# Retention and a low-rank mixer on one core: the low-rank expansion in four row tiles, later scores in batch 2, a later load of U

## The chip, the cores and the metric

The kernel runs on one core of one Trainium2 chip. The time is the device time of one execution in microseconds. The kernel before takes 241.34 us, the median of three runs (241.11 to 241.67).

## The reference, cut to what matters

There are 4 batches, 8 heads, 768 tokens and a head dimension of 64, so a token has 512 values. First comes a retention: each head has a state that decays by a factor of its own at each token, takes in the outer product of k and v, and is read with q. The heads side by side are x. Then a low-rank mixer works across tokens (U is 768 x 32, V is 32 x 768), and a feed-forward works on each token:

```python
state = gamma * state + einsum('bhd,bhe->bhde', k[:, :, t], v[:, :, t])
y[:, :, t] = scale * einsum('bhd,bhde->bhe', q[:, :, t], state)
# x: y with the heads side by side, (4, 768, 512)
h = x.transpose(0, 2, 1) @ U @ V
u = x + h.transpose(0, 2, 1)
out = u + np.maximum(u @ w_ch1, 0.0) @ w_ch2      # 512 -> 2048 -> 512
```

Inputs and output are float32.

## The kernel before, in words

**Retention.** The kernel takes the tokens in chunks of 128. GpSimd scales q and k of a chunk by powers of the decay and casts to bf16 (prep_chunk, L240 to L253). The chunk is turned so that the head dimension lies on partitions: for batch 1 by TensorE and a copy by ScalarE (turn_pe, L376), for batches 2 and 3 by one DMA transpose through the crossbar, issued from ScalarE's queue (turn_dma, L387 to L392; tile qkT). Then state (L394) updates the running state, score (L413) makes the products of q and k in two PSUM banks with the tag s, VectorE multiplies them with the causal mask (L422), and mix (L425) sums them with v and with the state into bank o, which ScalarE copies out as x. Score needs the turned chunk, mix needs both masked tiles. Batch 0 has a version of its own, before everything else.

**The low-rank part.** lr_proj (L450) multiplies x with U, giving for each of four column blocks c of 128 values a product of 32 x 128. The four lie on partitions 32c to 32c+31 of one tile, pc, which VectorE copies out of bank o. lr_expand (L460 to L470) multiplies it with V, block by block: for a token block j and a column block c it is one matmul with 32 rows of contraction (L464), and its row tile in the array is c. Before the change, a call does two column blocks, into two banks with the tag s, and then VectorE adds x to each bank (L468), giving u. A second call does the other two column blocks; it takes the same two banks, so it waits until VectorE has read them. u is turned for the feed-forward into uT, for batches 0 and 1 by TensorE (lr_turn_pe, L472, two token blocks at a time through bank qk, copied by ScalarE), except that blocks 0 to 3 of batch 0 are made directly at L632; for batches 2 and 3 by the crossbar (lr_turn, L481 to L484). Names in the trace: u_752, u_1515, u_2183 and u_2810 are batches 0 to 3.

**Feed-forward, and the order.** The feed-forward of a batch is a list of 56 pieces of four matmuls each (mlp_pieces, L496): 16 up pieces for tokens 0 to 511 (L507, priced 0.864), 16 up pieces for tokens 512 to 767 (priced 0.432), and 24 down pieces, four to each token block (L530, 0.864). The prices sum to 41.47. Up pieces end in a relu, the third of every three on VectorE, the others on ScalarE. While the feed-forward of batch b-1 is written out, the retention and the low-rank part of batch b are put between its pieces by weave (L551): each step has a mark, a share of the 41.47, and goes ahead of the first piece that begins at or after it. The marks are in L653 to L680: chunk i has a mark at[i], and turn, state, score and mix come at[i], at[i] + lag[0], + lag[1] and + lag[2]. After the last mix come projection, the expansion of token blocks 0 to 3, and their turns; blocks 4 and 5 follow at the start of the next batch (first, L638 and L650). Each engine runs its instructions in the order of this program.

**PSUM.** There are eight banks (L63): one each for the tags qk, o and st, two for s, three for the feed-forward.

**Loads.** All loads go through the sync queue in the order of the list feed (L138 to L155), 16 ahead of their use. U is needed twice, in a pair-wise order of tokens for batch 0 and in natural order for the others; the second (key u2) is loaded after the up weights, and prep_u2 (L263) has GpSimd cast U and copy V for it, ahead of batch 1's first chunk.

Of the kernel before, what the change touches and what calls it, by code (L numbers as in the profile page):

```python
# [17 lines left out]
def kernel(  # L18
# [11 lines left out]
    nc = tc.nc  # L30
    P = 128
# [6 lines left out]
    NCB = DM // P  # L38
# [26 lines left out]
    def bank(tag, dtype=fp32):  # L65
        n_bank[0] += 1
        return psum.tile([P, 2048 // (4 if dtype == fp32 else 2)], dtype,
                         tag=tag, name=f"{tag}_{n_bank[0]}", bufs=BANKS[tag])

    def four(t):  # L70
        return t.rearrange("p (n m) -> p n m", n=4)
# [21 lines left out]
    feed = []  # L93
# [3 lines left out]
    def feed_chunk(b, ci):  # L97
        for nm, src in (("q", q), ("k", k), ("v", v)):
            feed.append(((nm, b, ci),
                         src[b, :, ts(ci, P), :].rearrange("h p d -> p h d")))  # L100
# [8 lines left out]
    def feed_one():  # L109
        if n_fed[0] == len(feed):  # L110
            return
        key, src = feed[n_fed[0]]
        n_fed[0] += 1
        if key[0] == "uv":
            for i in range(2):
                nc.sync.dma_start(
                    out=Uf[0][ds(HP * i, HP)],
                    in_=moe_U.rearrange("(j p two) r -> two p j r", p=HP,
                                        two=2)[i])
            for c in range(NCB):  # L120
                nc.sync.dma_start(out=Vf[ds(RK * c, RK)], in_=moe_V)
            return
        if key[0] == "u2":
            nc.sync.dma_start(out=Uf[1],
                              in_=moe_U.rearrange("(j p) r -> p j r", p=P))
            return
        t = rin.tile([P, 512], fp32, tag="in", name=f"in_{n_fed[0]}")
        ready[key] = t
        if key[0] in "qkv":
            t = t.rearrange("p (h d) -> p h d", h=H if len(key) == 3 else 4)  # L130
        nc.sync.dma_start(out=t, in_=src)  # L131

    def take(*key):
        assert feed[n_used[0]][0] == key, (feed[n_used[0]][0], key)
        n_used[0] += 1
        return ready.pop(key, None)
# [4 lines left out]
    for mb in range(4):  # L141
        for c in range(NCB):
            feed.append((("w1", mb, c), moe_w_ch1[ts(c, P), ts(mb, 512)]))
    feed.append((("u2",), None))
    for ci in range(AHEAD):
        feed_chunk(1, ci)
    for m in range(NM):
# [1 line left out]
    for b in range(1, B):  # L149
        for ci in range(NCK):  # L150
            if b > 1 or ci >= AHEAD:
                feed_chunk(b, ci)
    for _ in range(RING):
        feed_one()

# [6 lines left out]
    def keep_busy(n, fresh=False):  # L162
        if fresh:
            idle_bank[0] = bank("mlp")
        for _ in range(n):
            nc.tensor.matmul(idle_bank[0], ones[:, :P], ones, start=True,  # L166
                             stop=True, skip_group_check=True)
# [43 lines left out]
    for i in range(NST):  # L211
        t = consts.tile([P, 4, P], bf16, name=f"state{i}")
# [27 lines left out]
    def prep_chunk(b, ci):  # L240
        qkd = rpre.tile([P, 2, H, D], bf16, tag="qkd", name=f"qkd_{b}_{ci}")
        vd = rpre.tile([P, H, D], bf16, tag="vd", name=f"vd_{b}_{ci}")
        pre[b, ci] = qkd, vd
        for t, nm, g in ((qkd[:, 0], "q", gq), (qkd[:, 1], "k", gk),
                         (vd, "v", None)):
            src = take(nm, b, ci).rearrange("p (h d) -> p h d", h=H)
            if g is None:
                nc.gpsimd.tensor_copy(out=t, in_=src)
            else:
                nc.gpsimd.tensor_tensor(  # L250
                    t, src, g[:, ci, :, None].to_broadcast([P, H, D]),
                    op=ALU.mult)
            feed_one()  # L253
# [9 lines left out]
    def prep_u2():  # L263
        take("u2")
        nc.gpsimd.tensor_copy(out=Ub[1], in_=Uf[1])
        nc.gpsimd.tensor_copy(out=V4[1], in_=Vf)
        feed_one()

    def prep_w1(mb):
        for c in range(NCB):  # L270
            nc.gpsimd.tensor_copy(out=w1b[:, c, ts(mb, 512)],
                                  in_=take("w1", mb, c))
            feed_one()
# [170 lines left out]
    us, uTs, pcs = {}, {}, {}  # L444
# [12 lines left out]
        pcs[b] = rmid.tile([P, P], bf16, tag="pc", name=f"pc_{b}")  # L457
        evac("D", pcs[b], p_p[:, :P])

    def lr_expand(b, c0, j0, nj):  # L460
        banks = [bank("s") for _ in range(2)]
        for j in range(j0, j0 + nj):
            for c in (c0, c0 + 1):
                nc.tensor.matmul(banks[c - c0][:, ts(j - j0, P)],  # L464
                                 V4[b > 0][ds(RK * c, RK), ts(j, P)],
                                 pcs[b][ds(RK * c, RK)], start=True, stop=True)
        for c in (c0, c0 + 1):
            nc.vector.tensor_tensor(  # L468
                us[b][:, ds(j0, nj), ts(c, P)], four(banks[c - c0])[:, :nj],
                xs[b][:, ds(j0, nj), ts(c, P)], op=ALU.add)  # L470

    def lr_turn_pe(b, j0):  # L472
# [78 lines left out]
    def weave(pieces, *tracks):  # L551
        total = sum(c for c, _ in pieces)
        marks = []
        for steps, start, end in tracks:
            for i, f in enumerate(steps):
                marks.append((total * (start + (end - start) * i / len(steps)),
                              f))
        marks.sort(key=lambda m: m[0])
        at = 0.0
        for cost, f in pieces:  # L560
            while marks and marks[0][0] <= at:
                marks.pop(0)[1]()
            late = len(stores)
            f()
            for _ in range(late):
                store()
            at += cost
        for _, f in marks:
            f()
        while stores:  # L570
            store()

    def part(f, *args):
        return lambda: f(*args)
# [4 lines left out]
    def x_turn(c):  # L579
        xT[c] = bank("mlp" if c < 3 else "s")  # L580
        for j in range(NLO):
            nc.tensor.matmul(xT[c][:, ts(j, P)], xs[0][:, j, ts(c, P)], ident,
                             start=(j == 0), stop=False, skip_group_check=True)
# [34 lines left out]
    mix_block(NSC - 1, "AD")  # L618
    for mb in range(4):
        prep_w1(mb)  # L620
    prep_u2()
    x_turn(3)
    idle_bank[0] = bank("s")
    keep_busy(2)
# [10 lines left out]
    for c in range(NCB):  # L635
        evac("AD"[c % 2], uTs[0][:, :NLO, c], four(xT[c]))
    keep_busy(3)
    first = [part(lr_expand, 0, 0, 4, 2), part(lr_expand, 0, 2, 4, 2),  # L638
             part(lr_turn_pe, 0, 4),
             part(lr_expand, 0, 0, 0, 4),  # L640
             part(lr_expand, 0, 2, 0, 4)]

    for ci in range(AHEAD):
        prep_chunk(1, ci)
# [2 lines left out]
    for b in range(1, B + 1):  # L647
        tracks = []
        if b > 1:
            first = [part(lr_expand, b - 1, 0, 4, 2),  # L650
                     part(lr_expand, b - 1, 2, 4, 2),
                     part(lr_turn_pe if b == 2 else lr_turn, b - 1, 4)]
        tracks.append((first, 0.02, 0.2))  # L653
        if b < B:
            if b == 1:
                at = [0.5, 0.6, 0.655, 0.715, 0.77, 0.825]
                lag = [0.01, 0.035, 0.065]
                turn = turn_pe
                for i in range(AHEAD, NCK):
                    tracks.append(([part(prep_chunk, b, i)], at[i] - 0.1, 1))  # L660
            else:
                for i in range(NCK):
                    prep_chunk(b, i)
                at = [0.06 + 0.11 * i for i in range(NCK)]
                lag = [0.1, 0.12, 0.2]
                turn = turn_dma
            for i in range(NCK):
                for f, d in ((turn, 0), (state, lag[0]), (score, lag[1]),
                             (mix, lag[2])):
                    tracks.append(([part(f, b, i)], at[i] + d, at[i] + d))  # L670
            t = at[-1] + lag[2]
            tracks += [([part(lr_open, b), part(lr_proj, b)], t + 0.02, t + 0.02),
                       ([part(lr_expand, b, 0, 0, 4),
                         part(lr_expand, b, 2, 0, 4)], t + 0.035, t + 0.055)]
            if b == 1:
                tracks.append(([part(lr_turn_pe, b, 0), part(lr_turn_pe, b, 2)],
                               t + 0.07, t + 0.09))
            else:
                tracks.append(([part(lr_turn, b, 0), part(lr_turn, b, 2)],
                               t + 0.075, t + 0.076))  # L680
        weave(mlp_pieces(b - 1), *tracks)
# [29 lines left out]
```

## Time and profile before

| what | value |
|---|---|
| time, median of three runs | 241.34 us |
| span of the profiled execution | 240.2 us |
| TensorE matmul busy | 224.9 us, 94% |
| TensorE weight loads, beside matmuls | 123.3 us, 51% |
| VectorE busy | 96.5 us, 40% |
| ScalarE busy | 86.7 us, 36% |
| GpSimd busy | 81.2 us, 34% |
| moved by DMA | 39.18 MB, mean 163 GB/s |

Busy shares are means over stages with different limits. TensorE is the engine that is nearly always busy, so its gaps and what ends them are to be looked for; a gap on another engine costs nothing unless TensorE waits for it. In the lines of the profile, a time in brackets is the engine's idle time ahead of an instruction, with what ended it. Batch 0's retention takes the first 28 us, its feed-forward up to about 87, that of batch 1 up to about 142, of batch 2 to about 194, and of batch 3 to the end.

### The profile page before, as it was taken

Reading aid. Unit: us, or ns where it says so; the run is one execution under the profiler, and the core shown is the slowest. Engines: PE = TensorE matmul, PEld = TensorE weight load, DVE = VectorE, ACT = ScalarE, POOL = GpSimd, SP = SyncE. Lnnn points to the kernel's source line nnn. Section 1 sums busy time; section 2 is a strip of 40 time slices with the busy share of each in tenths; the row PEclk is TensorE's granted clock in tenths of the full one; section 3 lists DMA queues with packets and bytes.
Section 4 is the critical chain, followed back from the end, with each engine's and each line's share of the span. In section 5 each row is a group of like instructions: output and inputs, shape, how many; then the busy total and the mean of one; then the engine's idle time right before and its main releaser. Section 6 shows DMA issues by size and latency. Waiting matters only on the chain.

```text
span 240.2 us, 4801 instructions
## 1 busy us (share of the span) xinstructions
PE 224.9 (94%) x1936; PEld 123.3 (51%) x1936; DVE 96.5 (40%) x179; ACT 86.7 (36%) x175; POOL 81.2 (34%) x121
## 2 busy tenths in 40 slices
PE   7898999999999779997989999999999999999993
PEld 3466544685565334465544434568444434584441
DVE  5577445323435523443333524444334533321221
ACT  3266453455463045554320004566210024460000
POOL 5542879688676664264644100000000000000000
PEclk9999999999999999999999999999999999999999
DMA  6997999999999999999999163422331342001112
GB/s 181 295 293 187 277 343 257 364 315 227 216 221 213 235 216 258 212 163 227 170 262 196 46 147 71 90 44 49 84 91 46 87 132 46 0 0 46 72 59 87
DMA packets 94630, 39.18 MB, mean 163 GB/s; under 512 B 78096, under 2 KB 87312, under 8 KB 94608
## 3 DMA queue, kind: packets, MB, share of 16 engines
q1 hardware_dynamic: 73008, 29.43, 54.1%
q10 hardware_dynamic: 21600, 9.44, 16.9%
q8 instruction: 15, 0.25, 0.4%
q14 instruction: 7, 0.06, 0.1%
HBM read 27.85 MB, written 6.29 MB: 142 GB/s over the span
## 4 chain that ended last, share of the span: by engine, by line
PE 74%; DMA 14%; DVE 3%; ACT 2%; SPq 2%; issue 2%; POOL 1%; ACTq 0%; DVEq 0%; POOLq 0%
DMA qkT_2_1830<-qkd_2_1633 3%; DMA in_186<-in_v_dram 3%; DMA qkT_4_2015<-qkd_4_1655 3%; DMA in_106<-in_q_dram 2%; SPq L131 2%; PE mlp_1375 L530 2%; PE mlp_2776 L530 1%; PE mlp_2149 L530 1%; PE mlp_2672 L530 1%; PE mlp_1273 L530 1%; PE mlp_1179 L530 1%; PE mlp_2637 L530 1%; PE mlp_1095 L530 1%; PE mlp_3215 L530 1%; PE mlp_3155 L530 1%
## 5 line engine op out<-in xcount | busy, mean ns | idle before, releaser
L507 PEld LDWEIGHTS <-w1b 128*128 128x128 bf16 x512 | 48.0, 98 | 33.4 <-issue 1.4
L530 PEld LDWEIGHTS <-gT_2906 128*128 128x128 bf16 x96 | 9.4, 98 | 11.1
L530 PEld LDWEIGHTS <-gT_1677 128*128 128x128 bf16 x96 | 8.7, 98 | 9.6
L530 PEld LDWEIGHTS <-gT_2313 128*128 128x128 bf16 x96 | 8.7, 98 | 9.6
L530 PEld LDWEIGHTS <-gT_852 128*128 128x128 bf16 x96 | 8.2, 98 | 7.2
L166 PE MATMUL mlp_199<-ones 128*128 128x512 bf16 x24 | 8.0, 478 | 1.4 <-DVE ones L159 1.4
L166 PEld LDWEIGHTS <-ones 128*128 128x128 bf16 x40 | 3.8, 110 | 5.7 <-issue 2.3
L464 PEld LDWEIGHTS <-V_84 32*128 32x128 bf16 x72 | 2.2, 92 | 7.1 <-issue 7.1
L514 ACT ACTIVATE gT_2906<-mlp_2907 128x512 bf16<-128x512 f32 x1 | 0.6, 597 | 10.8 <-PE mlp_2907 L507 10.8
L514 ACT ACTIVATE gT_2313<-mlp_2314 128x512 bf16<-128x512 f32 x1 | 0.6, 597 | 10.7 <-PE mlp_2314 L507 10.7
L530 PE MATMUL mlp_1375<-w2b,gT_852 128*128 128x512 bf16 x16 | 4.1, 380 | 0.0
L530 PE MATMUL mlp_1179<-w2b,gT_852 128*128 128x512 bf16 x16 | 4.1, 380 | 0.0
L530 PE MATMUL mlp_1452<-w2b,gT_852 128*128 128x512 bf16 x16 | 4.1, 380 | 0.0
L530 PE MATMUL mlp_2212<-w2b,gT_1677 128*128 128x512 bf16 x16 | 4.0, 381 | 0.0
L530 PE MATMUL mlp_2839<-w2b,gT_2313 128*128 128x512 bf16 x16 | 4.0, 381 | 0.0
L530 PE MATMUL mlp_1544<-w2b,gT_852 128*128 128x512 bf16 x16 | 4.0, 380 | 0.0
L530 PE MATMUL mlp_2045<-w2b,gT_1677 128*128 128x512 bf16 x16 | 4.0, 380 | 0.0
L530 PE MATMUL mlp_2672<-w2b,gT_2313 128*128 128x512 bf16 x16 | 4.0, 380 | 0.0
L530 PE MATMUL mlp_1273<-w2b,gT_852 128*128 128x512 bf16 x16 | 4.0, 380 | 0.0
L530 PE MATMUL mlp_1095<-w2b,gT_852 128*128 128x512 bf16 x16 | 4.0, 380 | 0.0
L530 PE MATMUL mlp_2149<-w2b,gT_1677 128*128 128x512 bf16 x16 | 3.8, 380 | 0.0
L530 PE MATMUL mlp_2776<-w2b,gT_2313 128*128 128x512 bf16 x16 | 3.8, 380 | 0.0
(906 smaller groups left out, 549.4 us busy)
## 6 DMA issues: line engine op xcount, KB each, us to landing
Vf<-in_moe_V_dram SPq DMA_DIRECT2D x4, 96.0 KB, 4.1
in_90<-in_k_dram SPq DMA_DIRECT2D x1, 256.0 KB, 3.0
in_92<-in_k_dram SPq DMA_DIRECT2D x1, 256.0 KB, 3.4
in_94<-in_q_dram SPq DMA_DIRECT2D x1, 256.0 KB, 4.4
in_96<-in_q_dram SPq DMA_DIRECT2D x1, 256.0 KB, 4.7
in_98<-in_v_dram SPq DMA_DIRECT2D x1, 256.0 KB, 5.1
in_100<-in_v_dram SPq DMA_DIRECT2D x1, 256.0 KB, 5.4
in_102<-in_k_dram SPq DMA_DIRECT2D x1, 256.0 KB, 5.7
```

Of the source, the lines that this page charges most:

```text
L131: nc.sync.dma_start(out=t, in_=src)
L166: nc.tensor.matmul(idle_bank[0], ones[:, :P], ones, start=True, stop=True, skip_group_check=True)
L464: nc.tensor.matmul(banks[c - c0][:, ts(j - j0, P)], V4[b > 0][ds(RK * c, RK), ts(j, P)], pcs[b][ds(RK * c, RK)], start=True, stop=True)
L507: nc.tensor.matmul(g_p[:, :sz], w1b[:, c, ts(m, P)], uTs[b][:, ds(j, nj), c], start=(c == 0), stop=(c == NCB - 1))
L514: nc.scalar.activation(gT[:, m, ds(lo, sz)], g_p[:, :sz], AF.Relu)
L530: nc.tensor.matmul(ch, gT[:, m, ts(j, P)], w2b[:, m], start=(m == 0), stop=(m == NM - 1))
```

## The change

There are three edits, and the number of instructions of each kind stays the same.

The low-rank expansion does all four column blocks in one call. Its matmuls go to four row tiles of the array in turn and write four banks: the two of tag s, and those of o and qk. The purpose is that four row tiles can work side by side and that no call has to wait for the banks of the one before it. The VectorE adds follow one another.

For batch 2 the lags are larger: state at 0.12, score at 0.17 and mix at 0.21 behind the turn, in place of 0.10, 0.12 and 0.20. The purpose is to have the scores of batch 2 come later behind the crossbar transposes that they read. Everything behind the last mix of this batch has its mark 0.01 later.

The natural-order U is loaded behind the chunks of batch 1, and its casts on GpSimd stand behind the last chunk of batch 1 instead of ahead of the first.

```diff
-    feed.append((("u2",), None))
     for ci in range(AHEAD):
         feed_chunk(1, ci)
...
             if b > 1 or ci >= AHEAD:
                 feed_chunk(b, ci)
+        if b == 1:
+            feed.append((("u2",), None))
...
-    def lr_expand(b, c0, j0, nj):
-        banks = [bank("s") for _ in range(2)]
+    def lr_expand(b, j0, nj):
+        banks = [bank(t) for t in ("s", "s", "o", "qk")]
         for j in range(j0, j0 + nj):
-            for c in (c0, c0 + 1):
-                nc.tensor.matmul(banks[c - c0][:, ts(j - j0, P)],
+            for c in range(NCB):
+                nc.tensor.matmul(banks[c][:, ts(j - j0, P)],
                                  V4[b > 0][ds(RK * c, RK), ts(j, P)],
                                  pcs[b][ds(RK * c, RK)], start=True, stop=True)
-        for c in (c0, c0 + 1):
+        for c in range(NCB):
             nc.vector.tensor_tensor(
...
-    prep_u2()
...
-    first = [part(lr_expand, 0, 0, 4, 2), part(lr_expand, 0, 2, 4, 2),
-             part(lr_turn_pe, 0, 4),
-             part(lr_expand, 0, 0, 0, 4),
-             part(lr_expand, 0, 2, 0, 4)]
+    first = [part(lr_expand, 0, 4, 2), part(lr_turn_pe, 0, 4),
+             part(lr_expand, 0, 0, 4)]
...
+                tracks.append(([prep_u2], at[-1] - 0.05, 1))
...
-                lag = [0.1, 0.12, 0.2]
+                lag = [0.12, 0.17, 0.21] if b == 2 else [0.1, 0.12, 0.2]
...
-                       ([part(lr_expand, b, 0, 0, 4),
-                         part(lr_expand, b, 2, 0, 4)], t + 0.035, t + 0.055)]
+                       ([part(lr_expand, b, 0, 4)], t + 0.035, t + 0.035)]
```

More of the change, by code (lines that the diff above doesn't have):

```diff
@@ L458, in lr_proj @@
         evac("D", pcs[b], p_p[:, :P])
-    def lr_expand(b, c0, j0, nj):
-        banks = [bank("s") for _ in range(2)]
+    def lr_expand(b, j0, nj):
+        banks = [bank(t) for t in ("s", "s", "o", "qk")]
         for j in range(j0, j0 + nj):
-            for c in (c0, c0 + 1):
-                nc.tensor.matmul(banks[c - c0][:, ts(j - j0, P)],
+            for c in range(NCB):
+                nc.tensor.matmul(banks[c][:, ts(j - j0, P)],
                                  V4[b > 0][ds(RK * c, RK), ts(j, P)],
                                  pcs[b][ds(RK * c, RK)], start=True, stop=True)
-        for c in (c0, c0 + 1):
+        for c in range(NCB):
             nc.vector.tensor_tensor(
-                us[b][:, ds(j0, nj), ts(c, P)], four(banks[c - c0])[:, :nj],
+                us[b][:, ds(j0, nj), ts(c, P)], four(banks[c])[:, :nj],
                 xs[b][:, ds(j0, nj), ts(c, P)], op=ALU.add)
@@ L649 @@
         if b > 1:
-            first = [part(lr_expand, b - 1, 0, 4, 2),
-                     part(lr_expand, b - 1, 2, 4, 2),
+            first = [part(lr_expand, b - 1, 4, 2),
                      part(lr_turn_pe if b == 2 else lr_turn, b - 1, 4)]
```

## The prediction

> **What bounds the kernel now.** Page first: TensorE is busy 224.9 of 240.2 us, no other compute engine over 40%, the granted clock is full in every slice. So only TensorE's 15.3 us of gaps, and busy time that is overhead, can be won. The view of waits, TensorE alone, names the gaps (times in total, count, longest):
>
> ```profile
> PE s_1922 L418 <- DMA qkT_2_1830<-qkd_2_1633: 1.6, 1, 1.6
> ...
> PE s_2077 L418 <- DMA qkT_4_2015<-qkd_4_1655: 1.2, 1, 1.2
> PE qk_1593 L476 <- ACT uT_1516 L75: 1.1, 1, 1.1
> PE s_1563 L464 <- DVE u_1515 L468: 0.8, 1, 0.8
> PE s_1832 L418 <- DMA qkT_1_1767<-qkd_1_1622: 0.6, 1, 0.6
> PE mlp_2907 L507 <- DMA uT_2811<-u_2810: 0.6, 1, 0.6
> PE mlp_2314 L507 <- DMA uT_2184<-u_2183: 0.5, 1, 0.5
> ```
>
> Two kinds matter: batch 2's scores (L418) wait 3.33 us in all for crossbar transposes (0.58 + 1.57 + 1.18 in the timeline), and the expansion (L464) waits for VectorE's adds (L468). The windows view puts the first kind in one stage, where DMA is busiest (columns: TensorE, weight loads, VectorE, ScalarE, GpSimd busy, clock, DMA share, GB/s):
>
> ```profile
> 103.00:123.00 20.00, 17.21 (x164) 11.64 (x164) 7.17 (x13) 8.46 (x22) 10.26 (x12) 1.00 1.34 194
> ```
>
> The timeline shows what one expansion costs the stream (batch 2, token blocks 0 to 3):
>
> ```profile
> 133.75 1.04 PE L530 MATMUL mlp_2212<-w2b,gT_1677 128*128 128x512 bf16 x4
> ...
> 134.72 0.23 PE L464 MATMUL s_2218<-pc_2210,V_84 32*128 32x128 bf16 x1
> ...
> 135.05 1.04 PE L530 MATMUL mlp_2212<-w2b,gT_1677 128*128 128x512 bf16 x4
> 135.22 0.69 DVE L468 TENSOR_TENSOR u_2183<-s_2218,x_1807 128x512 bf16<-128x512 f32 x1 [0.93 <-PE s_2219 L464]
> ...
> 136.87 1.90 PE L530 MATMUL mlp_2212<-w2b,gT_1677 128*128 128x512 bf16 x8
> ...
> 137.55 0.68 DVE L468 TENSOR_TENSOR u_2183<-s_2235,x_1807 128x512 bf16<-128x512 f32 x1
> 138.26 2.64 ACTq L482 DMA_TRANSPOSE uT_2184<-u_2183  x2
> ...
> 142.75 1.04 PE L507 MATMUL mlp_2314<-uT_2184,w1b 128*128 128x512 bf16 x4 [0.53 <-DMA uT_2184<-u_2183]
> ```
>
> Four 512-column matmuls stream in 0.86 us. The first half costs 135.05 - (133.75 + 0.86) = 0.44 us, the second 136.87 - (135.05 + 0.86) = 0.96, as it waits for the adds that free its two banks. And the next batch's first up piece comes 4.49 us after the crossbar transposes are issued.
>
> **What the Trainium skill says.** "TensorE: Matmul & The Clock Gate", The mechanism: matmuls in different row tiles of the array run together. The trace agrees: at L632 four 32-row matmuls into four banks start within 10 ns, each 0.39 us:
>
> ```profile
> 27.77 0.39 PE L632 MATMUL mlp_623<-V_83,pc_779 32*128 32x512 bf16 x1
> ...
> 27.78 0.38 PE L632 MATMUL s_737<-V_83,pc_779 32*128 32x512 bf16 x1
> ```
>
> "TensorEngine Tiling (Array Packing)", Key Properties: a change of tiling mode drains the array; fewer groups mean fewer drains. The trace fits (0.42 us of weight-load idle put down to issue before most such groups). "DMA: Bandwidth & Descriptors", Issuing engines are not separate DMA queues: all transfers share 16 engines. The trace agrees: batch 2's six crossbar transposes land after 4.5 to 8.0 us while loads run; batch 3's six, with the loads over, after 3.1 to 3.2.
>
> **The change part by part.**
>
> *1. Expansion, token blocks 0 to 3.* 16 matmuls in one group, 4 rounds of four row tiles, in place of two groups of 4 rounds of two. At one round per 0.06 us, as now, a group costs what the first half costs, 0.44; if four tiles went as two pairs, 0.66. I take 0.45.
> - Batch 0: now 36.48 - 36.05 = 0.43 and 38.23 - 37.34 = 0.88; after 0.45. **-0.86.** These rows aren't needed soon.
> - Batch 1: both halves come at one mark, and LT (the turn of u by TensorE, lr_turn_pe, L476) follows two down pieces later. Now the second half idles 0.85 and 0.39, and LT starts at 84.08. After, TensorE is ready at about 82.4, but LT needs all four adds: from 80.69, one per 0.61, the last over at 80.69 + 1.83 + 0.69 = 83.21. LT starts at 83.26: **-0.82**. The wait for VectorE takes over part of the gain; LT's two halves still share bank qk (1.1 us).
> - Batch 3: the four adds run without the 0.43 gap on VectorE, so the last ends at 186.55 + 2.52 = 189.07 where it ended at 189.56. The crossbar starts 0.49 earlier, and it sets the next batch's start: **-0.49**. TensorE's own saving of 0.95 ends as a longer wait there (0.57 to about 1.0).
> - Batch 2: the new lag moves projection and expansion one down piece later. Group at 134.72 + 0.86 = 135.58, adds 136.08 to 138.60, crossbar 0.37 later than now: **+0.37**. TensorE is ready at 135.58 + 0.33 + 6 x 0.864 = 141.1 and the data come at 143.1: the 0.5 wait becomes 2.0.
>
> *2. Expansion, blocks 4 and 5.* Two groups into one in each batch. Each costs 0.31 to 0.38 now (88.69 - 88.38 = 0.31); one group after, 0.33. **4 x -0.31 = -1.24.** Hidden: the adds, and LT one piece earlier.
>
> Banks o and qk, newly lent: o was just emptied by the copy to pc, which the expansion needs anyway; qk goes back to LT, which needs all adds anyway. No wait added.
>
> *3. Scores of batch 2 at +0.17, mix at +0.21* (shares of 41.47 us of pieces). Turns keep their marks. Counting pieces, score 1 comes 2.2 us later against its turn (wait 0.58), score 2 2.2 (wait 1.57), score 4 2.6 (wait 1.18). But the saved waits themselves stood between turn and score. From the end of the up piece ahead of turn 2, what lies on TensorE before score 2 is 8.2 us, against a landing of 8.0 about 0.1 later. Score 4: 8.1 against 7.3; score 1: 8.1 against 6.5. All fit, score 2 barely. The transposes come closer together (5.3 us apart where it was 6.1 to 7.3), so I leave 0.5 of the 3.33 standing (bounds 0 and 1.8). **-2.8.**
> New wait: between score 0 and mix 0 lies only one up piece, 0.86 us, where there were four; queued on VectorE ahead of the masks is the relu of the piece before. Counted from that piece's end: relu starts at 0.20, masks at 0.81 and 1.42, the second over at 2.10; TensorE reaches the mix at 1.29 and ends it at 2.27 where it would have at 1.52. **+0.75** (mix 5 of batch 1 shows the same with 0.24; bounds 0.25 and 0.9). The other mixes have at least 1.7 us between and don't wait.
>
> *4. U later.* GpSimd's two copies (0.35 + 0.83 us) leave 38.15 us, where nobody waits (TensorE waits for no weight cast), and come after batch 1's last chunk (71.9). The load follows that chunk's load (issued 66.2 to 67.3), and with its 5.5 us to landing the copies end by about 75; projection needs them near 77.5. Batch 2's first chunk slips by 2 to 3 us, 10 us before its turn. **0.**
>
> Sum: -0.86 - 0.82 - 0.49 + 0.37 - 1.24 - 2.8 + 0.75 = -5.1, so 241.34 - 5.1 = 236.2 us.
>
> **The rivals.**
> - *Crossbar-bound:* transposes land later as they crowd, 1.8 us of waits stay. For: DMA share 1.34, 8.0 us landings. Against: the later mix frees GpSimd's buffers later, which delays loads. -5.1 + 1.3 = -3.8: 237.5.
> - *Row tiles go in pairs:* 0.22 more for each of four large groups, 0.1 for each small one: +1.3, 237.5. Against: L632.
> - *Better:* VectorE's relu doesn't delay the masks (+0.25), no waits stay: -6.1, 235.2.
> - *Slower:* batch 2 is bound by DMA whatever the marks (the 3.33 stay, with 0.75 added) and U's load, 128-byte rows in traffic, takes 11 us, so that projection waits 3.2: -5.1 + 2.8 + 3.2 = +0.9, 242.2. For: its landing is shown once only, and batch 2's loads are issued back to back then. Against: POOL's copies have 2 us of slack, and the later marks do give the 8.0 us landings their time.
>
> **How the numbers follow.** Forecast 0.70, crossbar-bound 0.12, pairs 0.08, better 0.06, slower 0.04. The range takes in the bounds of the mix (0.5 lower), of remaining waits (0.5 lower, 1.3 higher) and of the group's cost (1.3 higher), not all at once: 234.9 to 238.3. A slower case at 0.04 and 0.03 for the others adding up to nothing: faster 0.93, same 0.03, slower 0.04.
>
> **What the profile after would show.** Right: L464 has four starts within some 10 ns, 8 groups in place of 16, and no wait for VectorE; LT of batch 1 waits about 0.9 for the fourth add; the waits of batch 2's scores sum to under 1; mix 0 of batch 2 waits some 0.7 for a mask; the first up piece of batch 2's output waits about 2 us for uT, that of batch 3's about 1; pc of batch 1 isn't held up by Ub. Wrong: crossbar transposes of batch 2 over 8.5 us to landing, group starts in pairs, or a wait for GpSimd before projection.

## The result, and the profile after

| | before | after |
|---|---|---|
| median of four executions, us | 241.5 (241.11 to 241.83) | 237.79 (236.65 to 238.47) |
| span of the profiled execution, us | 240.2 | 234.9 |
| TensorE matmul busy, us | 224.9 | 221.9 |

The ratio is 0.9842 [0.98, 0.9884]: 3.7 us faster. The two traces differ by 5.3 us, more than the medians. Most of what follows on sizes is about this difference.

The view of waits of the kernel after, TensorE alone (us in total, count, longest; the lines that belong to the change):

```profile
PE mlp L508 <- DMA uT<-u: 2.8, 2, 1.8
...
PE qk L477 <- ACT uT L75: 1.1, 1, 1.1
PE qk L477 <- DVE u L469: 0.8, 1, 0.8
...
PE mlp L508 <- ACT gT L515: 0.3, 1, 0.3
PE o L438 <- DVE a L423: 0.3, 1, 0.3
```

Two kinds of line are gone: the scores that wait for crossbar transposes (qkT), and the expansion that waits for VectorE. In their place stands, at the top, uT: the first up piece of batch 2's output waits 1.8 us and that of batch 3's 1.0 for the transposed u. LT of batch 1 (L477) waits 0.8 for the last add. All lines now are one number higher than before.

The windows view of the stage in which batch 2's scores lie, in the same stretch and with the same columns as in the prediction:

```profile
103.00:123.00 20.00, 19.62 (x176) 12.46 (x175) 8.30 (x15) 7.81 (x20) 10.68 (x12) 1.00 1.34 202
```

TensorE is busy 19.62 of 20 us where it was busy 17.21, while the DMA share is the same 1.34. The transfers are hardly faster: the crossbar transposes of q and k for batches 2 and 3 land after 4.2 us in the median and 7.5 at most, where it was 3.8 and 8.0. The scores come late enough for them.

The timeline of batch 2's expansion, tokens 0 to 511 (start, duration, engine, line, operation, and in brackets the idle time before it):

```profile
131.12 0.23 PE L465 MATMUL s<-pc,V 32*128 32x128 bf16 x2
131.13 0.23 PE L465 MATMUL o<-pc,V 32*128 32x128 bf16 x1
131.13 0.22 PE L465 MATMUL qk<-pc,V 32*128 32x128 bf16 x1
...
131.62 1.29 DVE L469 TENSOR_TENSOR u<-s,x 128x512 bf16<-128x512 f32 x2 [1.06 <-PE qk L465]
...
133.42 0.68 DVE L469 TENSOR_TENSOR u<-qk,x 128x512 bf16<-128x512 f32 x1
...
134.14 2.65 ACTq L483 DMA_TRANSPOSE uT<-u  x2
...
138.63 1.04 PE L508 MATMUL mlp<-uT,w1b 128*128 128x512 bf16 x4 [1.82 <-DMA uT<-u]
```

Four starts lie within 10 ns. After them the path to the next batch leaves TensorE: four adds in a row on VectorE up to 134.10, the crossbar transposes issued at 134.14, and the up piece 4.49 us later, as long as before. TensorE has nothing to do in the last 1.82 us of it.

The two halves of LT in batch 1 show the same kind of end, ahead of batch 2's feed-forward:

```profile
82.07 0.61 PE L477 MATMUL qk<-ident,u 128*128 128x128 bf16 x8 [0.80 <-DVE u L469]
83.79 0.61 PE L477 MATMUL qk<-ident,u 128*128 128x128 bf16 x8 [1.11 <-ACT uT L75]
```

And mix 0 of batch 2 waits for its second mask, with a piece following at 99.13:

```profile
98.41 0.29 PE L438 MATMUL o<-vd,a 128*128 128x64 bf16 x4
99.01 0.29 PE L438 MATMUL o<-vd,a 128*128 128x64 bf16 x4 [0.31 <-DVE a L423]
```

### The profile page after: what moved, and what is told of

Same layout as the page of the kernel before. It is cut to its first block, busy times and chain, and to the rows that moved or that the text cites. A ratio compares the mean times of both kernels' runs of the same rounds, so it can differ in the third digit from the quotient of the medians.

```text
span 234.9 us, 4801 instructions
## 1 busy us (share of the span) xinstructions
PE 221.9 (94%) x1936; PEld 122.4 (52%) x1936; DVE 95.9 (41%) x179; ACT 87.0 (37%) x175; POOL 81.1 (35%) x121
## 4 chain that ended last, share of the span: by engine, by line
PE 84%; DVE 5%; DMA 4%; ACT 3%; issue 1%; ACTq 1%; DVEq 0%
PE mlp L508 35%; PE mlp L531 30%; PE mlp L167 3%; DMA uT<-u 3%; PE s L419 2%; DVE u L469 2%; PE o L438 2%; PE mlp L293 1%; PE st L403 1%; DMA out_dram<-o 1%; PE o L433 1%; DVE o L536 1%; PE qk L383 1%; PE st L316 1%; PE qk L477 1%
## 5 line engine op out<-in xcount | busy, mean ns | idle before, releaser
L508 PE MATMUL mlp<-uT,w1b 128*128 128x512 bf16 (+1 forms) x512 | 88.5, 326 | 3.5 <-DMA uT<-u 2.8
L531 PE MATMUL mlp<-w2b,gT 128*128 128x512 bf16 x384 | 89.9, 380 | 0.0
L515 ACT ACTIVATE gT<-mlp 128x512 bf16<-128x512 f32 (+1 forms) x88 | 42.5, 490 | 58.9 <-PE mlp L508 47.8
L531 PEld LDWEIGHTS <-gT 128*128 128x128 bf16 x384 | 34.9, 98 | 37.3
L513 DVE TENSOR_SCALAR gT<-mlp 128x512 bf16<-128x512 f32 (+1 forms) x40 | 22.3, 557 | 44.6 <-PE mlp L508 44.1
L423 DVE TENSOR_TENSOR a<-s,mask 128x512 bf16<-128x512 f32 x36 | 23.2, 685 | 27.6 <-PE s L419 27.6
L536 DVE TENSOR_TENSOR o<-mlp,u 128x512 f32<-128x512 f32 x24 | 16.6, 690 | 42.8 <-PE mlp L531 42.8
L251 POOL TENSOR_TENSOR qkd<-in,gq 128x512 bf16<-128x512 f32 x18 | 18.8, 1042 | 16.0 <-DMA in<-in_q_dram 14.7
L251 POOL TENSOR_TENSOR qkd<-in,gk 128x512 bf16<-128x512 f32 x18 | 18.8, 1042 | 7.7 <-DMA in<-in_k_dram 7.3
L75 ACT ACTIVATE state<-st 64x256 bf16<-64x256 f32 x40 | 15.0, 375 | 7.9 <-PE st L316 3.8
L343 DVE TENSOR_TENSOR a<-s,mask 128x512 bf16<-128x512 f32 x10 | 6.4, 685 | 3.6 <-PE s L334 3.6
```

What stands on the lines that cost most here:

```text
L75: nc.scalar.activation(dst, src, AF.Copy)
L251: nc.gpsimd.tensor_tensor(t, src, g[:, ci, :, None].to_broadcast([P, H, D]), op=ALU.mult)
L423: nc.vector.tensor_tensor(a, four(sp[i]), causal(mask), op=ALU.mult)
L508: nc.tensor.matmul(g_p[:, :sz], w1b[:, c, ts(m, P)], uTs[b][:, ds(j, nj), c], start=(c == 0), stop=(c == NCB - 1))
L513: nc.vector.tensor_relu(gT[:, m, ds(lo, sz)], g_p[:, :sz])
L515: nc.scalar.activation(gT[:, m, ds(lo, sz)], g_p[:, :sz], AF.Relu)
```

## The experiments

The theory was that of the prediction: three independent gains (group and bank, scores, and nothing from U), each read from one trace. The main rivals were that the score waits in that trace were not typical, that a part is worth something only together with another, and, after the first runs, that the new waits cost clock.

In four of the traces below TensorE's granted clock is half of full for one stretch of 3.41 us in the middle of the work. Such a stretch lowers the mean granted clock of an execution by 0.007, so I call an execution with a mean below 0.995 one with a fall; of executions without a trace only the mean is known. The counts of these stand with each run, and the kernel before has 5 in 57.

**Tiles only.** The kernel after, with the lags and the place of U of before:

```diff
+    feed.append((("u2",), None))
     for ci in range(AHEAD):
         feed_chunk(1, ci)
...
+    prep_u2()
...
-                tracks.append(([prep_u2], at[-1] - 0.05, 1))
...
-                lag = [0.12, 0.17, 0.21] if b == 2 else [0.1, 0.12, 0.2]
+                lag = [0.1, 0.12, 0.2]
```

> Only the expansion in four row tiles; lags and U as before. Theory (the sum of the prediction): batch 0 -1.2, batch 1 -1.1, batches 2 and 3 -0.8 each, so 3.9 us less than before, with the score waits of batch 2 (3.3 us) still in the view of waits, no wait of a first up piece over 1.1 us, and executions that agree within 0.3% as before. Rival (the spread of the changed kernel comes from the expansion itself): the same mean gain but executions spread over 1.5 us or more.

Measured: 238.43 us, 0.9874 [0.9845, 0.9904], falls in 2 of 6. Between medians that is -2.6, not -3.9. The six spread over 2.9 us, but so do the 35 of the kernel before beside them without their slowest one (239.56 to 242.45), so this does not show that the expansion brings the spread. The waits of this kernel (a trace with a fall) show the two for uT that the theory allowed for, and one that it had not put there:

```profile
PE mlp L507 <- DMA uT<-u: 1.9, 2, 1.0
...
PE st L402 <- POOL vd L248: 1.2, 1, 1.2
```

TensorE reaches batch 1's retention earlier, as batch 0's expansion is shorter, and finds GpSimd late by 1.2 us. That takes back the whole of batch 0's -0.86 here. It is not this edit's own, though: the kernel before, taken again below, waits 0.8 at the same place, and in its first trace not at all.

**Lags only.** The kernel before with the new lags:

```diff
-                lag = [0.1, 0.12, 0.2]
+                lag = [0.12, 0.17, 0.21] if b == 2 else [0.1, 0.12, 0.2]
```

> Only the later lags of batch 2; expansion and U as before. Theory: score waits of 3.3 us gone, mix 0 +0.75, ScalarE's late relu +0.3, both expansion halves now back to back one piece later (+0.85 on the crossbar turn of u), so 1.4 us less than before. Rival (crossbar-bound): transposes land later, over 1 us of score waits stay, and the gain is under 0.5 us.

Measured: 241.19 us, 1.0015 [0.9995, 1.0035], 14 executions, falls in 4. Nothing is gained, though the score waits are gone from the trace. In their place (total, count, longest):

```profile
PE s L464 <- DVE u L468: 3.0, 6, 0.9
...
PE mlp L507 <- ACT gT L514: 0.4, 1, 0.4
PE o L437 <- DVE a L422: 0.3, 1, 0.3
```

The trace of the kernel before taken again, below, has 2.1 us on the first of these lines. The up-to-up stretch of batch 2 (from the first up piece of batch 1's output to that of batch 2's) takes 54.1 us here. With the old lags and the old expansion it takes 55.2 in the trace that the prediction read, 53.6 in that repeat and 54.9 in the next experiment's trace. Less the score waits of each (3.3, 1.6 and 3.1) these three are 51.9, 52.0 and 51.8. So the new lags take the score waits away and lengthen the stretch by 2.2 us elsewhere: they can pay only in an execution whose score waits sum to more than that, as they did in that first trace.

**U only.** The kernel before with the load of U behind batch 1's chunks and its casts ahead of the last one, as in the change's first and last hunks:

```diff
-    feed.append((("u2",), None))
...
+        if b == 1:
+            feed.append((("u2",), None))
...
-    prep_u2()
...
+                tracks.append(([prep_u2], at[-1] - 0.05, 1))
```

> Only the later load and casts of U; expansion and lags as before. Theory: within 0.3 us of before, no wait of TensorE on GpSimd. Rival (loads moved by U shift the crossbar transposes of batch 2): the score waits change by more than 0.5 us and so does the time.

Measured: 241.21 us, 0.9999 [0.9981, 1.0017], 22 executions, a fall in 1. The step "0" holds by itself.

**Tiles and lags, U as before.** The kernel after, with only the move of U undone: its load ahead of batch 1's chunks and its casts in batch 0:

```diff
+    feed.append((("u2",), None))
     for ci in range(AHEAD):
         feed_chunk(1, ci)
...
+    prep_u2()
     x_turn(3)
...
-                tracks.append(([prep_u2], at[-1] - 0.05, 1))
```

> Expansion and lags of the changed kernel, U loaded where it was before. Theory: same as the changed kernel within 0.3 us, 3.7 to 5.1 us less than before. If executions spread between 236.6 and 238.5 again, U has no part in the spread. Rival (U's casts in front of batch 2's chunks cause the spread): executions agree within 0.3%, about 5 us less than before.

Measured: 238.17 us, 0.9888 [0.9867, 0.991], falls in 4 of 6, against 0.9874 for the tiles alone and 0.9842 for the whole; the intervals overlap. TensorE waits 0.4 us for GpSimd in batch 1. The trace shows a fall where the new uT wait is. Timeline, then windows (TensorE, weight loads, VectorE, ScalarE, GpSimd, clock, DMA share, GB/s):

```profile
139.44 1.04 PE L507 MATMUL mlp<-uT,w1b 128*128 128x512 bf16 x4 [1.85 <-DMA uT<-u]
...
140.64 4.61 PE L507 MATMUL mlp<-uT,w1b 128*128 128x512 bf16 x13
```

```profile
138.00:140.70 2.70, 1.26 (x13) 0.49 (x14) 0.32 (x1) 0.12 (x1) 0.00 (x0) 0.98 0.85 256
140.70:144.10 3.40, 3.40 (x10) 1.21 (x10) 1.42 (x4) 1.07 (x2) 0.00 (x0) 0.52 0.08 15
144.10:147.00 2.90, 2.90 (x15) 1.27 (x14) 0.89 (x2) 1.19 (x2) 0.00 (x0) 1.00 0.39 73
```

From 140.7 to 144.1 TensorE is busy throughout, but starts 10 matmuls in 3.4 us where the next stretch starts 15 in 2.9. This batch's up pieces take 26.39 us where the kernel after, without a fall, takes 24.76: the fall costs 1.6 us. The guess from it was that the 1.8 us wait for uT brings the fall, and that a shorter wait would end it.

**The adds in halves.** The kernel after, with the adds of two token blocks of all four banks first, so that each transpose of u can start after half the work:

```diff
-        for c in range(NCB):
-            nc.vector.tensor_tensor(
-                us[b][:, ds(j0, nj), ts(c, P)], four(banks[c])[:, :nj],
+        for h in range(0, nj, 2):
+            for c in range(NCB):
+                nc.vector.tensor_tensor(
+                    us[b][:, ds(j0 + h, 2), ts(c, P)],
+                    four(banks[c])[:, ds(h, 2)],
...
```

> The changed kernel, with the adds of token blocks 0 to 3 in two halves: first blocks 0 and 1 of all four banks, then 2 and 3, so that the first turn of u starts after four short adds. Theory (the four adds in a row set the turn): the turn of batch 1 starts 0.85 earlier without a wait for VectorE, the first up pieces of batches 2 and 3 come 1.0 us earlier each, so 2.8 us less than the changed kernel, about 6.2 us less than before. Clock theory (the long wait at a batch's end makes the granted clock fall to half for one stretch of 3.4 us in some executions): with waits of uT at 0.8 us or less, mean granted clocks under 0.995 become rare, where the changed kernel's parts had 12 in 30. Rival (the falls come from elsewhere): as many as before the halves.

Measured: 235.98 us, 0.9759 [0.9711, 0.9808], falls in 4 of 6. The boundaries of batches 2 and 3 are each 1.0 us shorter than after (from the first down piece to the next first up piece 25.80 for 26.83 and 24.69 for 25.76), as expected. The waits for uT are 0.8 in one place in all. But falls did not end. This trace's fall lies elsewhere, after batch 1's LT:

```profile
81.49:84.90 3.41, 1.28 (x18) 1.05 (x19) 0.95 (x3) 1.04 (x2) 1.32 (x2) 1.00 1.05 228
84.90:88.31 3.41, 3.41 (x16) 1.00 (x14) 0.69 (x1) 1.21 (x2) 2.13 (x3) 0.50 1.03 215
```

Here TensorE idled twice for 1.1 us within 2.8 us (LT waits for the last add, then for ScalarE's copy), and was busy 1.28 of the 3.41 us before the clock fell. So the guess that the uT wait alone brings the falls fell with this run. The falls in the traces of the tiles only (at 85.87) and of tiles and U (at 84.18, below) lie at this place as well. Halved adds do not shorten LT's first wait, because LT writes bank qk, which the last add still reads: 0.85 of the 2.8 us expected did not come.

**Marks 0.01 earlier.** The kernel after, with batch 2's chunks as a whole earlier:

```diff
-                at = [0.06 + 0.11 * i for i in range(NCK)]
+                at = [(0.05 if b == 2 else 0.06) + 0.11 * i for i in range(NCK)]
```

> The changed kernel, with the marks of batch 2 starting at 0.05 in place of 0.06. Theory: projection and expansion go back by one down piece and mix 0 has two up pieces behind score 0, so the wait of batch 3's... of batch 2's first up piece falls from 1.8 to about 1.0 (0.86 us less time there), and 0.75 us of mask wait goes: 1.6 us less than the changed kernel, if the transposes of batch 2 still land in time. Rival (the lag's cost at the end of batch 2 isn't real): no change.

Measured: 235.56 us, 0.9748 [0.9705, 0.9791], no fall in 6. The longest wait for uT is 1.0 where it was 1.8, and the mix of batch 2 no longer waits for a mask. Batch 1's LT waits 0.8 and 1.1 as before, so these two alone did not bring a fall here in six executions.

**Tile by tile.** The kernel after, with the matmuls of one column block issued together, so that in order of issue no two neighbours are in different row tiles except at three places:

```diff
-        for j in range(j0, j0 + nj):
-            for c in range(NCB):
+        for c in range(NCB):
+            for j in range(j0, j0 + nj):
```

> The changed kernel with the expansion's two loops exchanged: all matmuls of one row tile, then the next tile. Theory (four row tiles run side by side, a round of four costs what one matmul costs): the 16 matmuls become 16 rounds of 0.056 us, a large group costs 1.1 us in place of 0.45, a small one 0.7 in place of 0.33. Large groups of batches 1 to 3 hide that in the waits that follow; batch 0's and the four small ones don't: 0.67 + 4 x 0.34 = 2.0 us more than the changed kernel. Rival (tiles go in pairs or one by one anyway): less than 0.7 us more.

Measured: 237.62 us, 0.9817 [0.9755, 0.988], no fall in 4: no difference from the kernel after that these runs can show. Its timeline, batch 0:

```profile
36.19 0.24 PE L465 MATMUL s<-pc,V 32*128 32x128 bf16 x2
36.22 0.23 PE L465 MATMUL o<-pc,V 32*128 32x128 bf16 x1
36.23 0.22 PE L465 MATMUL qk<-pc,V 32*128 32x128 bf16 x1
36.26 0.23 PE L465 MATMUL s<-pc,V 32*128 32x128 bf16 x2
...
36.56 2.76 PE L508 MATMUL mlp<-uT,w1b 128*128 128x512 bf16 x12
```

The first matmuls of banks o and qk are the ninth and thirteenth of the group in the program. They start 30 and 40 ns after the first matmul, and ahead of the second ones of the s banks. The group takes 0.36 us to the next piece, against 0.33 in the kernel after. So the row tiles fill side by side in either order, and the theory that the new order in turn makes the gain was wrong. What is left is that one group stands where two stood and that no group waits for a bank: 16 matmuls in four tiles take 0.33 us from their start to the next piece, as 8 in two tiles did (135.05 - 134.72).

**The kernel before again.** No edit; one execution.

> The kernel before once more, for its trace on this chip. Theory that the lags' gain is small because the score waits of batch 2 vary from execution to execution: the waits for crossbar transposes sum to 1.0 to 2.5 us here where the first trace had 3.3. Rival (the waits are always 3.3 us, and the later lags lose as much elsewhere): 3.0 us or more.

Measured: 240.77 us, one execution, span 239.0. Its waits:

```profile
PE s L464 <- DVE u L468: 2.1, 5, 0.8
PE s L418 <- DMA qkT<-qkd: 1.6, 1, 1.6
...
PE st L402 <- POOL vd L248: 0.8, 1, 0.8
```

The scores wait 1.6 us here and 3.33 in the first trace, with the same program. The other traces with the old lags have 2.3 (tiles only), 3.1 (U only) and 3.1 (tiles and U).

**Halves, earlier marks, another bank.** The two previous gains together, and the first half of batch 1's LT in bank st, so that it needs not wait for the add that reads bank qk:

```diff
...
-    def lr_turn_pe(b, j0):
-        tp = bank("qk", bf16)
+    def lr_turn_pe(b, j0, tag="qk"):
+        tp = bank(tag, bf16)
...
-                tracks.append(([part(lr_turn_pe, b, 0), part(lr_turn_pe, b, 2)],
+                tracks.append(([part(lr_turn_pe, b, 0, "st"), part(lr_turn_pe, b, 2)],
...
```

> The changed kernel with the adds in halves, batch 2's marks from 0.05, and batch 1's first turn of u in bank st, so that it waits neither for the last add to free qk nor the second turn for ScalarE's copy. Theory: batch 1's end 1.4 us shorter, batch 2's 1.0 (halves) + 0.86 + 0.75 (marks), batch 3's 1.0: 5.0 us less than the changed kernel, near 232.5, with waits of uT under 0.3 us and hardly any mean clock under 0.995. Rival (gains overlap or the transposes of batch 2 catch up): 234.5 or more.

Measured: 232.28 us (230.97 to 232.71), 0.9636 [0.9598, 0.9674], no fall in 6. It beats both kernels. No wait for uT stands in its view, and LT's two waits of 0.8 and 1.1 have become one:

```profile
PE qk L479 <- DVE u L470: 0.6, 1, 0.6
```

**The waits filled.** The kernel after, with matmuls of ones ahead of the waiting instructions; they add work that nobody uses and take no wait away (the last line is ahead of the first up piece of a batch):

```diff
+                tracks.append(([part(fill, 3), part(lr_turn_pe, b, 0),
+                                part(fill, 4), part(lr_turn_pe, b, 2)],
...
+        if b in (2, 3):
+            fill(7 if b == 2 else 4)
```

> The changed kernel with matmuls of ones, read by nobody, laid into the waits ahead of batch 1's turns (3 and 4) and of the first up pieces of batches 2 and 3 (7 and 4); each lot is shorter than the wait it lies in. Clock theory (idle time at a batch's end makes the clock fall): mean clocks under 0.995 vanish, the median falls by the share of the falls, 0.5 to 0.9 us, and the span without a fall is unchanged. Rival (falls don't come from idle time): as many falls as in the changed kernel.

Measured: 236.91 us, 0.9855 [0.9814, 0.9896], no fall in 6. Its span in the trace, 234.8, is that of the kernel after, 234.9, so the filling cost nothing there. On the same chip the kernel after has a fall in three of six; six executions of each are few, and the two intervals overlap.

**The kernel after again.** No edit.

> The changed kernel again, beside the others on this chip. Clock theory: mean clocks under 0.995 in a third or more of the executions, these about 1 us slower than the rest. Rival: none.

Measured: 238.19 us (236.7 to 239.17), 0.9883 [0.9841, 0.9925]. The executions without a fall took 236.7, 236.78 and 239.13; those with one 238.18, 238.2 and 239.17. One without is as long as the longest with one, and so is one of the filled kernel (239.25): a second source of spread that no trace here caught.

**Tiles and U, lags as before.** The kernel after, with only the lag line undone:

```diff
-                lag = [0.12, 0.17, 0.21] if b == 2 else [0.1, 0.12, 0.2]
+                lag = [0.1, 0.12, 0.2]
```

> The changed kernel with the lags of before in batch 2: four row tiles and the later U alone. Theory (score waits here are about 1.6 us, not 3.3, and the later lags give 0.34 back at the end of batch 2, 0.75 at mix 0 and 0.3 at ScalarE): within 0.5 us of the changed kernel, with score waits of 1.5 to 2.5 us and an uT wait of 1.0 in batch 2. And it is about 1 us less than tiles alone, as batch 1 no longer waits for GpSimd. Rival (the lags are worth the 2 us of the prediction): 2 us more than the changed kernel.

Measured: 238.78 us, 0.9898 [0.9853, 0.9943], falls in 4 of 6. Beside the repeat of the kernel after on the same chip the lags bring 0.6 us between medians, and the intervals overlap. The trace has score waits of 3.1 us, and waits of 1.0 + 1.0 for uT instead of 1.8 + 1.0. No wait for GpSimd stands in it, yet the time is not below that of the tiles alone (0.9874), where about 1 us less was expected.

## Why the prediction was right, and which terms were off

The direction and the range were right: 237.79 lies in 234.9 to 238.3, 1.6 us above the 236.2 named. Step by step, by the stretches between the first up and the first down pieces in the two first traces (no fall in either):

| stretch | predicted, us | measured, us |
|---|---|---|
| batch 0's expansion and blocks 4, 5 | -0.86 - 0.31 | -1.20 |
| batch 1's expansion | -0.82 | -0.86 |
| batch 2: blocks 4, 5, scores, mix 0, expansion later | -0.31 - 2.8 + 0.75 + 0.37 | -2.11 |
| blocks 4, 5 behind it | -0.31 | -0.31 |
| batch 3's expansion | -0.49 | -0.54 |
| blocks 4, 5 behind it | -0.31 | -0.31 |
| sum | -5.1 | -5.3 |

- *Expansion.* 0.33 us from the group's start, four starts within 10 ns, LT waiting 0.8 for the last add (0.9 foretold): right. The saving in TensorE's own time at batches 2 and 3 did reappear as a wait for uT, 1.82 and 1.0 us (2 and 1 foretold). Group to up piece in batch 2 was 142.75 - 134.72 = 8.03 and is 138.63 - 131.12 = 7.51; one piece later, 0.86, makes the +0.34 for the +0.37 foretold.
- *The reason given for it* was half right: the tiles work side by side, but the order in turn has no part in it (tile by tile costs the same). "TensorE: Matmul & The Clock Gate", The mechanism, has tiles running together, and the trace agrees: four starts within 10 ns. It also has matmuls start strictly in the order of issue; tile by tile the trace differs, with the ninth and thirteenth ahead of the second.
- *Mix 0*: 0.75 foretold. TensorE goes from 98.15, the end of its up piece, to 99.13, where the eight matmuls alone cost 0.23: 0.75.
- *Not foreseen*: one up piece of batch 2 waits 0.32 us for a relu (gT), which stands on ScalarE's queue behind the issue of crossbar transposes that moved up to it. It is inside the -2.11.

Two terms were off, and that the time lies in the range owes something to luck: the upper part of the range was there for row tiles in pairs and for score waits that stay, and neither came. Taken again, the change gave 2.4 us of the 5.1 foretold. As a rough split, the executions of after without a fall have a median of 236.8, 0.6 us over the forecast, and I put that down to the first term; what the median of all four lies above it, 1.0, I put down to the second. These are five executions from two sets, beside which the kernel before took 241.5 and 240.56.

1. *The scores, -2.8.* The step took the waits of one trace, 3.33 us, as the price of the old lags. Four other traces with these lags show 1.6, 2.3, 3.1 and 3.1. Their sum is a draw; in the profiled execution of before it was the highest of the five, and that execution was also slower (240.2 us of span, 239.0 in the repeat). And the cost of the new lags was put too low: 0.75 + 0.37 in the sum, against about 1.5 with the tiles (-2.11 + 0.31 + 3.33 in the table; the late relu is 0.3 of it) and 2.2 without them. Without the tiles the lags gave nothing (1.0015), with them 0.6 us between medians, with intervals that overlap. So the table's -2.11 rests on the first trace's draw, and within the noise of these runs the tiles alone (0.9874) make the gain of the whole (0.9842, and 0.9883 taken again).
2. *The clock, not in the sum at all.* The kernel after has a fall in 5 of 10 executions, the kernel before in 5 of 57. The five without one have a median of 236.8, the five with one 238.2: 1.4 us apart, in which the trace of the kernel with tiles and lags, 1.6 us longer in the one stretch, agrees.

That the idle time itself brings the fall is supported and not proved. Filling the waits left the spans as they were and gave no fall in six; the kernel that has only 0.6 us of them left gave none in six; all four traces with a fall show it begin within 1.2 us of the end of a wait, three behind batch 1's LT and one behind the wait for uT. "TensorE: Matmul & The Clock Gate", Part 1, has the clock follow how busy TensorE has lately been, in windows of some 3.4 us whose start is not tied to the program, and come down after an idle one. The traces agree on the windows: in all fourteen, every change of the granted clock lies a whole number of steps of 3.413 us behind the first clock record (the four falls 23, 23, 23 and 39 steps), and that record starts anywhere from 4.4 to 7.5 us into the span. How the waits lie in these windows is then a draw, which would explain why only some executions have a fall. These are the two emptiest such windows in the middle of the kernel after; no fall follows either:

```profile
81.53:84.94 3.41, 1.76 (x20) 1.28 (x20) 0.49 (x1) 1.53 (x2) 2.23 (x3) 1.00 0.99 234
136.14:139.56 3.42, 1.60 (x8) 0.41 (x5) 0.69 (x1) 0.00 (x0) 0.00 (x0) 1.00 0.99 258
```

But no window ahead of a fall was idle: TensorE was busy 1.28, 1.49, 1.50 and 1.56 of 3.41 us in the four. Windows without a fall behind them come down to 1.60 here, to 1.58 with the earlier marks, and to 1.48 in one at the very end of the kernel before. So the busy time in the window nearly separates the two kinds, and the line between them stays open. Against a simple rule stands the kernel with the lags only: it had a fall in 4 of 14, though the emptiest window in the middle of its trace, which has no fall there, is busy 2.19 us. The earlier marks and the tile-by-tile order kept batch 1's waits, the latter the 1.8 us too, and gave no fall in ten together.

*U*: right at 0 alone, and in the combination the medians show nothing: 238.17 without the move, 237.79 and 238.19 with it, and the intervals overlap. GpSimd holds TensorE up in batch 1 in some traces, with the old place of U (1.2, 0.8, 0.4 us) and once with the new (1.0, the earlier marks), so these waits can't be put down to it.

The rivals fell. "Row tiles in pairs" by the four starts; "crossbar-bound" by a stage in which no score waits; "slower" by the result, though its premise, that landings vary, is the one that was underrated. The figure that the first two gave, 237.5, is near the measured time for other reasons.

## What to carry to other kernels

Before you price a wait on a shared resource, look at more than one execution: its sum here went from 1.6 to 3.3 us in the same program. When work ahead of a fixed latency is made shorter on one engine, follow the chain to the next engine: here four adds in a row and a 4.49 us transfer kept the gain as a wait, and splitting the adds, setting batch 2's marks 0.01 earlier and freeing one bank brought 232.28 us, a gain of 8.3 us on its chip where the change alone gave 2.4 beside it. Waits that lie close together may cost a second time in the clock after them, so try to spread or fill them, and read the clock of every execution and not only that of the traced one.

## What was not expected of the hardware

- A stretch of half clock, 3.41 us long (140.57 to 143.98 and 84.90 to 88.31 in two traces, granted 0.50), came in all four traces behind a window in which TensorE was busy less than 1.6 of 3.41 us. Executions with one took 1.4 us longer between medians, and a batch's up pieces 1.6 us longer in one trace.
- Small matmuls of different row tiles run side by side without being issued in turn: the thirteenth of sixteen issued started 40 ns after the first. 16 of them in four tiles cost 0.33 to 0.36 us in either order, as much as 8 in two tiles.
